# A change to the order of loads, small vector work and stream tiles in the up stage of one token block of an attention and SwiGLU kernel

## The chip, the cores and the metric

The kernel runs on one NeuronCore of a Trainium2 chip. The core has a matrix engine (TensorE, PE), a vector engine (VectorE, DVE), a scalar engine (ScalarE, ACT), GpSimd (POOL) and SyncE (SP). SP computes nothing here: it issues nearly all DMA transfers, one after another, and 16 DMA engines carry them. The metric is the device time of one execution in microseconds (us), the median of several runs. Lower is better.

## What is computed

An attention without softmax: for each batch and head k^T v is formed over the sequence, q is multiplied by it, and each row of 64 is normalised by its root mean square. Its output is regrouped to 4608 tokens of 512 and goes through a SwiGLU feed-forward block. All in float32.

```python
def _attn_ref(q, k, v, g_norm):            # 8 batches, 8 heads, 576 positions, 64 wide
    kv = np.einsum('bhsd,bhse->bhde', k, v)
    out = np.einsum('bhsd,bhde->bhse', q, kv)
    rms = np.sqrt(np.mean(out * out, axis=-1, keepdims=True) + 1e-06)
    return out / rms * g_norm

x = attn_out.transpose(0, 2, 1, 3).reshape(4608, 512)
g = x @ w_gate                             # 512 x 1536
silu = g * (1.0 / (1.0 + np.exp(-g)))
y = (silu * (x @ w_val)) @ w_out           # 1536 x 512
```

## The kernel before, in words

**Blocks.** The 4608 tokens are nine blocks of 512. An object `Att(n)` makes the input x of block n from q, k, v, and an object `Ffn(n)` carries it through an up stage (gate and value products), the SwiGLU product and a down stage. Nine blocks of 512 cover eight batches of 576, so block n needs the k^T v of batch n and of batch n - 1.

**Fast matrix products.** The large products use Strassen's scheme in Winograd's form: seven products of quarter blocks in place of eight, with sums of the operands before and of the products after. Block 0 multiplies plainly, while its weights arrive. Block 1 (`Up`) uses one level. Block 2 (`Inner`) and the pairs of blocks 3 and 4, 5 and 6, 7 and 8 (`Joint`) use two levels in the up stage, 49 leaf products, each named by an outer and an inner number such as (5, 1). The down stages (`Down`) use one level.

**Streamed weights.** Sums of weights (the leaves) are computed once in block 1 (`leaf_steps`, L922 and after) and written to a DRAM tile `w` by `send` (L932). Block 2 takes 16 of the 49 leaves straight from the gate and value weights that lie in SBUF (`RESIDENT`, `QUARTER`); the other 33 it streams from `w`. The pairs stream all 49. A stream tile is one buffer of `t_pool`, which has nine. `ALONE` (L841) lists in which tiles, and in which order, block 2 loads its leaves: 17 tiles for each of the three thirds d of the up stage. Where the leaves of a tile lie side by side in `w`, one transfer of 256 KB loads them (L894); otherwise two transfers of 128 KB do (L897). In the list before, 10 of the 17 tiles need two, which makes 27 transfers per third. `Stream.pump` (L878) adds a load whenever the ninth tile before it is free again.

**Queues.** The order of the instructions on each engine is settled when the kernel is built. The builder may move independent instructions past one another; `tc.issue_after` and `tc.keep_in_program_order` tie some of them. After that each engine works through its own list in order, and waits on semaphores where data or a buffer are not ready. For SP this means that a transfer that waits holds all transfers behind it.

**Units of the up stage of block 2.** Four units for each third (`Inner.GROUPS`: outers (1, 5), (6, 2), (7,), (4, 3)), twelve in all; units and tiles are counted from 0. In `Ffn.up` every unit runs its seven inner products; the last two of a unit (3 and 4) fall into the next one. After unit i the function `fill[i + 1]` is called: this is where attention work for later blocks is placed. `ahead` (L1230) makes this table for block 2. Products land in PSUM pools a, b, c (1, 3 and 2 buffers), and VectorE (L132) or ScalarE (L775) move them into ring tiles r.

**Attention work of block 3.** It consists of `load_kv(g)` (four transfers of 288 KB for half of the heads, L294), `kv(g)` (36 pairs of 64x64 matmuls, L344, then copies by ScalarE, L351), `load_quarters(i, pairs)` (q in pieces of 24 to 40 KB, L312; a block is 32 such pieces), `turn_q` (a transposition on VectorE, L359), `heads` (q times k^T v, L389), `squares` (squares on ScalarE, L402, and sums on VectorE, L403), `root` (the inverse root by an integer guess and three Newton steps on VectorE, L409 to L421), `scale` (L134), `turn_x` (transpositions on TensorE, L436, with copies on ScalarE, L437) and `sums` (four operand sums on VectorE). Loads of q, k and v share `ld_pool`, four buffers.

**Where it stands before.** k, v half 0 of block 3 is loaded at the end of block 1's up stage. All of q follows after block 1's down stage (`load_q`, L312). In `ahead`, unit 0 is followed by the first k, v product and the load of half 1; `turn` comes after unit 2, the second k, v product after unit 3, the halves of the attention product after units 4 and 7. k, v and q of block 4 are loaded in between. In the pairs, `fill` places the k, v products of the next two blocks after units 5 and 12, and the loads of their q after units 13 to 20.

Of the kernel before, what the change touches and what calls it, by code (L numbers as in the profile page):

```python
# [18 lines left out]
def kernel(  # L19
# [194 lines left out]
    class Att:  # L214
# [118 lines left out]
        def kv(self, g):  # L333
# [4 lines left out]
            if g == 0:  # L338
                self.kv_ps = [m_psum.tile([P, 2, D], F32, name="m") for _ in range(2)]
# [8 lines left out]
            if g == 1:  # L348
                dst = kvs[self.n % 3].rearrange("p (g r) d -> p r g d", r=2)
                for r in range(2):  # L350
                    nc.scalar.copy(out=dst[:, r], in_=self.kv_ps[r])  # L351
# [27 lines left out]

        def heads(self, i, pairs, pools=None):  # L380
# [14 lines left out]
        def squares(self, i):  # L395
            if self.z is None or 0 < self.n < TURNED:
                self.z = st_pool.tile([P, 2, 2, 2, NS], F32, name="z")
            if i == 0:
                self.sq = self.place("sq").rearrange("p f (t j d) -> p f t j d", t=2, j=NS)
            for u in range(2):  # L400
# [4 lines left out]
        def root(self, i, k=1):  # L405


# [9 lines left out]
            y, a, z = flat(y), flat(a), flat(z)  # L417
            for _ in range(3):
                nc.vector.scalar_tensor_tensor(out=a, in0=y, scalar=-0.5, in1=y, op0=OP.mult, op1=OP.mult)
                nc.vector.tensor_tensor(out=a, in0=a, in1=z, op=OP.mult)  # L420
                nc.vector.scalar_tensor_tensor(out=y, in0=a, scalar=1.5, in1=y, op0=OP.add, op1=OP.mult)  # L421

        def scale(self, i):
            if i == 0:
                self.xts = self.place("xts").rearrange("p (i t) (j u d) -> p i t j u d", i=2, j=NS, u=2)
            for u in range(2):
# [3 lines left out]
        def turn_x(self, i):  # L430
            xt = self.xts[:, i].rearrange("p t j u d -> p t j (u d)")
            for j in range(0, NS, 2):
                ps = m_psum.tile([P, 2, 2, P], F32, name="m")
                for e in range(2):
                    for t in range(2):
                        nc.tensor.transpose(ps[:, e, t], xt[:, t, j + e], ident)  # L436
# [31 lines left out]
        def sums(self):  # L468

            a11, a12, a21, _, s1, s3, s4 = (self.x[:, i] for i in range(7))  # L470
            add(nc.vector, s1, a21, self.x[:, 3])
            sub(nc.vector, s3, a21, a11)
            sub(nc.vector, a21, s1, a11)
            sub(nc.vector, s4, a12, a21)
# [332 lines left out]
    class Joint(Inner):  # L807
# [116 lines left out]

    def leaf_steps(j, sources, room):
# [8 lines left out]
        for t, os in sources:  # L934
# [9 lines left out]
            yield lambda t=t, os=os: send(os, (1, 6, 2, 3), t.rearrange("p o i e c -> p o (i e c)"))  # L944
# [93 lines left out]
    class Ffn:  # L1038
        def __init__(self, n, att):
# [4 lines left out]
            self.making, self.later, self.latest = [], [], []  # L1044
            self.visited = None
# [19 lines left out]
        def up(self, fill):  # L1065
# [11 lines left out]
            for i, this in enumerate(units):  # L1077
                if i + 1 < len(units):
                    units[i + 1].prepare()
                for unit, p in this.sequence(last):  # L1080
                    if unit:
# [3 lines left out]
                        self.make(4)  # L1085
                last = this
# [135 lines left out]
    def visit(ffn, att, gs):  # L1222

        with tc.issue_after(ffn.multiplied.ins):
            for g in gs:
                att.kv(g)
# [3 lines left out]
    def ahead(ffn, att):  # L1230

        def start():
            visit(ffn, att, (0,))
            att.load_kv(1)

        def turn():
            att.turn()
            blocks[PAIRED + 1].load_kv(0)

        def finish():  # L1240
            visit(ffn, att, (1,))
            blocks[PAIRED + 1].load_kv(1)

        def half(i):
            with tc.issue_after(ffn.multiplied.ins):
                att.half(i, (m_psum, m_psum))
            ffn.visited = att.multiplied

        def load(i):
            blocks[PAIRED + 1].load_quarters(i // 2, (i % 2,))  # L1250

        def second():
            visit(ffn, blocks[PAIRED + 1], (0, 1))
            load(0)

        def last():
            half(1)
            load(1)

        def turn_x(i):  # L1260
            with tc.issue_after(ffn.multiplied.ins):
                att.turn_x(i)
            load(2 + i)
            if i == 1:
                att.sums()
# [4 lines left out]
        }  # L1270
        return {
# [127 lines left out]
```

## Time and profile before

| | |
|---|---|
| three runs | 1039.46, 1039.88, 1041.76 us; median 1039.88 |
| profiled execution | 1040.75 us, of which 1039.0 from its first to its last instruction (the span) |
| mean granted TensorE clock | 0.989 of full speed |
| DMA | 155.2 MB in 261349 packets, 141968 of them under 512 bytes |
| SP's queue | 53.3% of the time of 16 DMA engines; ScalarE's queue 2.4% |
| stream loads | 198 of 256 KB, median 3.2 us from issue to landing; 117 of 128 KB, 3.5 us |
| k and v loads | 26 and 26 of 288 KB, median 5.5 and 6.5 us |
| chain that ended last | TensorE 70% of the span, DMA 3%, SP's queue 2%, VectorE 1% |

Block 1's down stage ends at about 270 us, block 2's up stage runs from there to 373 us and its down stage to 416 us; the three pairs take the rest. The chain that ended last goes back from the last instruction, at each step to what released it. Its shares are over the whole span, so a wait of some microseconds in one stage hardly shows in them; it shows in views cut to that stage. In those views a line names an engine, a source line, the operation, the tile written and the tiles read; in brackets is the idle time before it and what ended that.

### The profile page before, as it was taken

To read this page: it belongs to the slowest core of one execution; us is meant where nothing else is said; L and a number is where in the kernel's file an instruction comes from. 1 tells how busy PE (TensorE), PEld (TensorE's weight loads), DVE (VectorE), ACT (ScalarE), POOL (GpSimd) and SP (SyncE) were. 2 spreads that over 40 slices of the span, in tenths; PEclk is the share of its full clock that TensorE was granted. 3 is DMA by queue.
4 is the path that set the end of the run, shared out by engine and by line. 5 is a ranking of instruction groups with operands and counts; after the bars stand their busy time and mean duration, and the time that the engine had idled before them with its cause. 6 is when DMAs were issued, how large, how long until landed. Compare 5 with 4: busy or idle time off the path is not lost.

```text
span 1039.0 us, 17769 instructions
## 1 busy us (share of the span) xinstructions
PE 998.8 (96%) x6774; PEld 843.6 (81%) x6774; DVE 685.2 (66%) x1166; ACT 228.6 (22%) x355; POOL 359.6 (35%) x283
## 2 busy tenths in 40 slices
PE   6999999999948989999999999999999999999998
PEld 4544688888938978888878888888888888888887
DVE  3999688887726696656668557566685566676311
ACT  2765112221102211211121111221212112111100
POOL 0000263534004451255445301455552024656600
PEclk9999999999969999999999999999999999999999
DMA  8689633777889656584761555566603555543011
GB/s 233 207 257 256 127 67 138 246 229 175 255 187 224 155 140 142 159 218 133 187 162 47 127 103 159 144 180 177 146 11 73 112 155 161 147 144 108 1 41 41
DMA packets 261349, 155.20 MB, mean 149 GB/s; under 512 B 141968, under 2 KB 240528, under 8 KB 261264
## 3 DMA queue, kind: packets, MB, share of 16 engines
q1 hardware_dynamic: 230544, 150.13, 53.3%
q10 hardware_dynamic: 30656, 3.94, 2.4%
q8 instruction: 54, 0.88, 0.4%
q14 instruction: 31, 0.25, 0.1%
q0 software_dynamic: 64, 0.00, 0.0%
HBM read 117.97 MB, written 28.70 MB: 141 GB/s over the span
## 4 chain that ended last, share of the span: by engine, by line
PE 70%; DMA 3%; SPq 2%; DVE 1%; issue 0%; ACT 0%; DVEq 0%; ACTq 0%
PE b L761 23%; PE b L593 16%; PE c L761 11%; PE c L593 8%; PE a L761 6%; PE a L593 4%; DMA t<-w 2%; PE m L389 1%; PE m L344 1%; SPq L312 1%; DVE r L132 1%; DMA out_dram<-r 1%; SPq L897 0%; DVE arena L134 0%; SPq L294 0%
## 5 line engine op out<-in xcount | busy, mean ns | idle before, releaser
L761 PE MATMUL b<-arena,t 128*128 128x256 f32 (+1 forms) x1248 | 281.8, 365 | 21.9 <-DMA t<-w 15.3
L761 PEld LDWEIGHTS b<-arena,t 128*128 128x128 f32 x1248 | 223.1, 193 | 53.0 <-DMA t<-w 10.6
L132 POOL TENSOR_TENSOR r<-r 128x256 f32<-128x256 f32 (+1 forms) x105 | 110.5, 1054 | 333.2 <-DMA t<-w 148.7
L132 DVE TENSOR_TENSOR r<-b,r 128x512 f32<-128x512 f32 (+1 forms) x273 | 162.4, 606 | 77.1 <-PE b L761 72.1
L132 DVE TENSOR_TENSOR r<-c,r 128x512 f32<-128x512 f32 (+1 forms) x179 | 109.2, 618 | 98.0 <-PE c L761 48.7
L761 PE MATMUL c<-arena,t 128*128 128x256 f32 (+1 forms) x624 | 140.0, 362 | 0.7 <-ACT r L775 0.7
L133 POOL TENSOR_TENSOR t<-wo 128x512 f32<-128x512 f32 x54 | 77.4, 1458 | 167.5 <-DVE wo L132 104.4
L132 DVE TENSOR_TENSOR r<-a,r 128x512 f32<-128x512 f32 (+1 forms) x99 | 62.5, 631 | 107.9 <-PE a L593 66.6
L134 POOL TENSOR_TENSOR arena<-r 128x1024 f32<-128x1024 f32 (+1 forms) x46 | 96.1, 2103 | 87.7 <-DVE r L132 75.9
L761 PEld LDWEIGHTS c<-arena,t 128*128 128x128 f32 x624 | 111.9, 193 | 14.3 <-ACT r L775 1.2
L133 DVE TENSOR_TENSOR arena<-arena 128x512 f32<-128x512 f32 (+3 forms) x101 | 102.4, 1026 | 18.2 <-PE b L593 12.1
L593 PE MATMUL b<-wo,arena 128*128 128x256 f32 x432 | 98.8, 382 | 2.3 <-DVE arena L134 1.5
L593 PE MATMUL b<-t,arena 128*128 128x256 f32 x432 | 96.3, 380 | 0.0
L593 PEld LDWEIGHTS b<-wo,arena 128*128 128x128 f32 x432 | 81.1, 190 | 13.9 <-DVE arena L134 1.8
L593 PEld LDWEIGHTS b<-t,arena 128*128 128x128 f32 x432 | 82.0, 190 | 11.4 <-POOL s L132 0.2
L775 ACT COPY r<-b 128x512 f32<-128x512 f32 x63 | 36.9, 585 | 215.4 <-PE b L761 214.7
L761 PE MATMUL a<-arena,t 128*128 128x256 f32 (+1 forms) x288 | 72.6, 371 | 0.9 <-DMA t<-w 0.9
L761 PEld LDWEIGHTS a<-arena,t 128*128 128x128 f32 x288 | 53.5, 194 | 7.7 <-PE c L761 1.3
L788 ACT ACTIVATE r<-r 128x1024 f32<-128x1024 f32 x21 | 22.2, 1057 | 120.9 <-DVE r L132 120.9
L593 PE MATMUL a<-wo,arena 128*128 128x256 f32 x216 | 48.4, 379 | 0.0
L593 PE MATMUL c<-wo,arena 128*128 128x256 f32 x216 | 48.1, 379 | 0.0
L593 PE MATMUL c<-t,s 128*128 128x256 f32 x216 | 48.1, 379 | 0.0
(118 smaller groups left out, 1134.6 us busy)
## 6 DMA issues: line engine op xcount, KB each, us to landing
t<-w SPq DMA_DIRECT2D x198, 256.0 KB, 3.2
t<-w SPq DMA_DIRECT2D x117, 128.0 KB, 3.5
out_dram<-r SPq DMA_DIRECT2D x17, 512.0 KB, 2.9
ld<-in_k_dram SPq DMA_DIRECT2D x26, 288.0 KB, 5.5
ld<-in_v_dram SPq DMA_DIRECT2D x26, 288.0 KB, 6.5
ld<-in_moe_w_gate_dram SPq DMA_DIRECT2D x12, 512.0 KB, 4.9
ld<-in_moe_w_val_dram SPq DMA_DIRECT2D x12, 512.0 KB, 4.7
ld<-in_moe_w_out_dram SPq DMA_DIRECT2D x12, 512.0 KB, 4.7
```

The source lines that it names most:

```text
L132: add = lambda e, o, a, b: e.tensor_tensor(out=o, in0=a, in1=b, op=OP.add)
L133: sub = lambda e, o, a, b: e.tensor_tensor(out=o, in0=a, in1=b, op=OP.subtract)
L134: mul = lambda e, o, a, b: e.tensor_tensor(out=o, in0=a, in1=b, op=OP.mult)
L312: nc.sync.dma_start(out=to[32 * r : 32 * (r + 1), j, g0:g1], in_=q[b, 4 * i + 2 * j + h, s0 : s0 + 32 * (g1 - g0), 32 * d : 32 * (d + 1)]. ...
L344: self.positions = nc.tensor.matmul(self.kv_ps[r][u * D : (u + 1) * D, g, :], lhsT=k[:, u, c, :], rhs=v[:, u, c, :], start=(c == 0), stop= ...
L389: self.multiplied = nc.tensor.matmul(self.ps[i][u][p : p + D, t, j, :], lhsT=self.qt[rows, 2 * i + t, j, p : p + D], rhs=kvs[b % 3][rows, ...
L593: self.ffn.multiplied = nc.tensor.matmul(banks[e][:, e], lhsT=lhsT, rhs=rhs, start=first and i == 0 and (e == 0 or banks[0] is not banks[1 ...
L761: self.ffn.multiplied = nc.tensor.matmul(to, lhsT=weight, rhs=self.operand(o, p), start=begins, stop=True, skip_group_check=True,)
L775: nc.scalar.copy(out=dst, in_=ps)
L788: nc.scalar.activation(out=c11, in_=c11, func=ACT.Silu)
```

## The change

Block 3's k, v half 1 is loaded at the end of block 1 in place of q. In block 2's up stage the table of `ahead` is new: both k, v products of block 3 after unit 0 (`visits`), its q in four parts after units 0 to 3, the k, v halves of block 4 loaded after units 1 and 4 and multiplied separately after units 4 and 10 (`apart`), the attention product's halves after units 5 and 7, the q of block 4 in four parts after units 5 to 8. VectorE's small steps are put in a list, `chores`, of which one is taken after every inner product: the transpositions of q, squares, root and scale, and the sums of x. `ALONE` groups the leaves so that 14 of its 17 tiles load with one transfer: 20 transfers per third. Four of the leaf writes of 512 KB (base leaves of the last two of six weight groups) go to a list `owed_sends` and are issued after unit 10. In the pairs `fill` places the k, v products after units 4 and 10 and the q loads after units 11 to 18.

```diff
@@ -330,12 +330,12 @@
-        def kv(self, g):
+        def kv(self, g, apart=False):
-            if g == 0:
+            if g == 0 or apart:
                 self.kv_ps = [m_psum.tile([P, 2, D], F32, name="m") for _ in range(2)]
...
-            if g == 1:
+            if g == 1 or apart:
                 dst = kvs[self.n % 3].rearrange("p (g r) d -> p r g d", r=2)
+                of = slice(g, g + 1) if apart else slice(0, 2)
                 for r in range(2):
-                    nc.scalar.copy(out=dst[:, r], in_=self.kv_ps[r])
+                    nc.scalar.copy(out=dst[:, r, of], in_=self.kv_ps[r][:, of])
@@ -377,6 +378,15 @@
+        def chores(self, i):
+            yield lambda: self.squares(i, (0,))
+            yield lambda: self.squares(i, (1,))
+            yield from self.root_steps(i)
+            for u in range(2):
+                yield lambda u=u: self.scale(i, (u,))
@@ -392,18 +402,28 @@
-        def squares(self, i):
+        def squares(self, i, us=(0, 1)):
-            if i == 0:
+            if i == 0 and us[0] == 0:
                 self.sq = self.place("sq").rearrange("p f (t j d) -> p f t j d", t=2, j=NS)
-            for u in range(2):
+            for u in us:
                 sq = self.sq[:, 2 * i + u]
                 self.squared = nc.scalar.activation(out=sq, in_=self.ps[i][u], func=ACT.Square)
                 self.summed = nc.vector.tensor_reduce(out=self.z[:, i, u], in_=sq, axis=mybir.AxisListType.X, op=OP.add)
         def root(self, i, k=1):
+            for step in self.root_steps(i, k):
+                step()
+        def root_steps(self, i, k=1):
+            yield lambda: self.guess(i, k)
+        def guess(self, i, k):
...
+            self.near = flat(y), flat(a), flat(z)
+        def refine(self):
+            y, a, z = self.near
+            nc.vector.scalar_tensor_tensor(out=a, in0=y, scalar=-0.5, in1=y, op0=OP.mult, op1=OP.mult)
+            nc.vector.tensor_tensor(out=a, in0=a, in1=z, op=OP.mult)
+            nc.vector.scalar_tensor_tensor(out=y, in0=a, scalar=1.5, in1=y, op0=OP.add, op1=OP.mult)
+        def scale(self, i, us=(0, 1)):
...
-            for u in range(2):
+            for u in us:
                 y = self.y[:, i, u].unsqueeze(3).to_broadcast([P, 2, NS, D])
                 self.scaled = mul(nc.vector, self.xts[:, i, :, :, u], self.ps[i][u], y)
@@ -433,7 +456,7 @@
-                        nc.tensor.transpose(ps[:, e, t], xt[:, t, j + e], ident)
+                        self.turned_x = nc.tensor.transpose(ps[:, e, t], xt[:, t, j + e], ident)
@@ -467,11 +490,16 @@
         def sums(self):
+            for step in self.sum_steps():
+                step()
+        def sum_steps(self):
             a11, a12, a21, _, s1, s3, s4 = (self.x[:, i] for i in range(7))
-            add(nc.vector, s1, a21, self.x[:, 3])
-            sub(nc.vector, s3, a21, a11)
-            sub(nc.vector, a21, s1, a11)
-            sub(nc.vector, s4, a12, a21)
+            yield lambda: add(nc.vector, s1, a21, self.x[:, 3])
+            yield lambda: sub(nc.vector, s3, a21, a11)
+            yield lambda: sub(nc.vector, a21, s1, a11)
+            yield lambda: sub(nc.vector, s4, a12, a21)
@@ -839,9 +867,9 @@
     ALONE = (
-        ((5, 1), (5, 6)), ((1, 5), (5, 5)), ((5, 2), (5, 3)), ((1, 7), (5, 7)), ((2, 5), (6, 5)), ((1, 4), (5, 4)),
-        ((2, 7), (6, 7)), ((7, 1), (7, 6)), ((7, 7), (7, 5)), ((2, 4), (6, 4)), ((7, 2), (7, 3)), ((4, 1), (4, 6)),
-        ((4, 5), (3, 5)), ((7, 4),), ((4, 2), (4, 3)), ((4, 7), (3, 7)), ((4, 4), (3, 4)),
+        ((5, 1), (5, 6)), ((1, 5), (5, 5)), ((5, 2), (5, 3)), ((5, 7), (5, 4)), ((1, 7), (1, 4)), ((2, 5), (6, 5)),
+        ((6, 7), (6, 4)), ((2, 7), (2, 4)), ((7, 1), (7, 6)), ((7, 5),), ((7, 2), (7, 3)), ((7, 7), (7, 4)),
+        ((4, 1), (4, 6)), ((4, 5), (3, 5)), ((4, 2), (4, 3)), ((4, 7), (4, 4)), ((3, 7), (3, 4)),
     )
@@ -922,6 +950,8 @@
+    owed_sends = []
     def leaf_steps(j, sources, room):
...
-            yield lambda t=t, os=os: send(os, (1, 6, 2, 3), t.rearrange("p o i e c -> p o (i e c)"))
+            base = lambda t=t, os=os: send(os, (1, 6, 2, 3), t.rearrange("p o i e c -> p o (i e c)"))
+            if os[0] in RESIDENT and j >= NP - 2:
+                owed_sends.append(base)
+            else:
+                yield base
             yield lambda b11=b11, t2_=t2_, to=to: sub(nc.vector, to[:, :, 0], b11, t2_)
             yield lambda to=to, os=os: send(os, (7, 4, 5), to.rearrange("p o r c -> p o (r c)"))
@@ -1042,6 +1076,7 @@
+            self.chores = []
@@ -1083,6 +1118,8 @@
                         with tc.issue_after(visited.ins) if visited else ExitStack():
                             unit.multiply(p)
                         self.make(4)
+                        if self.chores:
+                            self.chores.pop(0)()
                 last = this
                 fill.get(12 * (i + 1) // len(units), lambda: None)()
@@ -1219,58 +1256,60 @@
-    def visit(ffn, att, gs):
+    def visit(ffn, att, gs, apart=False):
         with tc.issue_after(ffn.multiplied.ins):
             for g in gs:
-                att.kv(g)
+                att.kv(g, apart)
         if att.n < B:
             ffn.visited = att.positions
-    def ahead(ffn, att):
-        def start():
-            visit(ffn, att, (0,))
-            att.load_kv(1)
+    def ahead(ffn, att, then):
+        def visits():
+            visit(ffn, att, (0, 1))
+            att.load_quarters(0, (0,))
+        def second():
+            att.load_quarters(0, (1,))
+            then.load_kv(0)
         def turn():
-            att.turn()
-            blocks[PAIRED + 1].load_kv(0)
-        def finish():
-            visit(ffn, att, (1,))
-            blocks[PAIRED + 1].load_kv(1)
+            visit(ffn, then, (0,), True)
+            then.load_kv(1)
+            ffn.chores += [lambda i=i: att.turn_q(i) for i in range(2)]
         def half(i):
             with tc.issue_after(ffn.multiplied.ins):
-                att.half(i, (m_psum, m_psum))
+                att.heads(i, range(NS), (m_psum, m_psum))
             ffn.visited = att.multiplied
-        def load(i):
-            blocks[PAIRED + 1].load_quarters(i // 2, (i % 2,))
-        def second():
-            visit(ffn, blocks[PAIRED + 1], (0, 1))
-            load(0)
-        def last():
-            half(1)
-            load(1)
+            ffn.chores += att.chores(i)
+            then.load_quarters(i, (0,))
         def turn_x(i):
             with tc.issue_after(ffn.multiplied.ins):
                 att.turn_x(i)
-            load(2 + i)
+            ffn.visited = att.turned_x
             if i == 1:
-                att.sums()
+                ffn.chores += att.sum_steps()
+        def last():
+            visit(ffn, then, (1,), True)
+            while owed_sends:
+                owed_sends.pop(0)()
...
         }
+        def again(i):
+            then.load_quarters(i, (1,))
         return {
-            1: start, 3: turn, 4: finish, 5: lambda: half(0), 7: second, 8: last, 9: lambda: turn_x(0),
-            10: lambda: turn_x(1),
+            1: visits, 2: second, 3: lambda: att.load_quarters(1, (0,)), 4: lambda: att.load_quarters(1, (1,)),
+            5: turn, 6: lambda: half(0), 7: lambda: again(0), 8: lambda: half(1),
+            9: lambda: (turn_x(0), again(1)), 10: lambda: turn_x(1), 11: last,
         }
@@ -1316,7 +1355,7 @@
-            ffn.up(ahead(ffn, nxt))
+            ffn.up(ahead(ffn, nxt, blocks[PAIRED + 1]))
@@ -1325,8 +1364,7 @@
         if n == 1:
-            for i in range(2):
-                blocks[PAIRED].load_q(i)
+            blocks[PAIRED].load_kv(1)
@@ -1351,9 +1389,9 @@
-            fill = {6: first_kv, 13: second_kv}
+            fill = {5: first_kv, 11: second_kv}
             for i in range(8):
-                fill[14 + i] = lambda i=i, after=after: after[i // 4].load_quarters(i % 4 // 2, (i % 2,))
+                fill[12 + i] = lambda i=i, after=after: after[i // 4].load_quarters(i % 4 // 2, (i % 2,))
```

More of the change, by code (lines that the diff above doesn't have):

```diff
@@ L405, in root @@
         def root(self, i, k=1):
+            for step in self.root_steps(i, k):
+                step()
+        def root_steps(self, i, k=1):
+            yield lambda: self.guess(i, k)
+            for _ in range(3):
+                yield self.refine
+        def guess(self, i, k):
             z = self.z[:, i : i + k]
@@ L416, in root @@
             flat = lambda t: t.rearrange("p i u t j -> p (i u t j)")
[L417 to L424, printed above, removed]
+            self.near = flat(y), flat(a), flat(z)
[5 more added lines that the diff above has]
+        def scale(self, i, us=(0, 1)):
+            if i == 0 and us[0] == 0:
                 self.xts = self.place("xts").rearrange("p (i t) (j u d) -> p i t j u d", i=2, j=NS, u=2)
-            for u in range(2):
+            for u in us:
                 y = self.y[:, i, u].unsqueeze(3).to_broadcast([P, 2, NS, D])
```

## The prediction

> **What bounds the kernel now.** I read the page's first two parts, then one call of busy time by stretches, the waits of TensorE, the timelines of SP and TensorE, and the rows of the stream loads. The page:
>
> ```profile
> PE 998.8 (96%) x6774; PEld 843.6 (81%) x6774; DVE 685.2 (66%) x1166; ACT 228.6 (22%) x355; POOL 359.6 (35%) x283
> ...
> PE   6999999999948989999999999999999999999998
> PEclk9999999999969999999999999999999999999999
> ```
>
> TensorE is busy 96% of 1039.0 us, and the two slices in which it is not lie at 285 to 310 us, where the clock falls too. That is the up stage of block 2, from 270 to 373 us, the stage that the diff rewrites. Busy time by stretches there (PE, weight loads, DVE, ACT, POOL, then clock, DMA share, GB/s):
>
> ```profile
> 270.00:285.00 15.00, 14.51 (x189) 14.13 (x187) 9.15 (x15) 2.34 (x4) 1.59 (x3) 1.00 0.78 235
> 285.00:310.00 25.00, 9.29 (x45) 8.78 (x46) 6.16 (x9) 1.06 (x1) 1.32 (x2) 0.59 0.79 182
> 310.00:329.00 19.00, 19.00 (x284) 18.62 (x283) 12.07 (x24) 4.92 (x9) 10.07 (x6) 1.00 1.10 250
> 329.00:340.00 11.00, 7.61 (x175) 7.20 (x174) 6.19 (x13) 1.49 (x3) 2.43 (x4) 0.84 0.60 168
> 340.00:361.00 21.00, 21.00 (x243) 20.81 (x242) 15.40 (x33) 6.71 (x11) 10.58 (x7) 1.00 0.63 148
> 361.00:373.00 12.00, 9.69 (x80) 9.09 (x79) 11.86 (x21) 1.26 (x2) 3.98 (x4) 1.00 0.77 188
> ```
>
> Idle is 103 minus 81.1 busy, or 21.9 us. What ended it, by TensorE's waits from 270 to 373 us:
>
> ```profile
> PE b L761 <- DMA t<-w: 15.3, 2, 10.4
> PE b L761 <- DVE r L132: 6.6, 5, 3.4
> ```
>
> Two waits for streamed weights, five for VectorE's evacuations. SP's queue says why the weights were late:
>
> ```profile
> 275.98 0.43 SPq L1049 DMA_DIRECT2D out_dram<-r  x1
> 276.47 17.26 SPq L312 DMA_DIRECT2D ld<-in_q_dram  x30
> 293.82 0.92 SPq L897 DMA_DIRECT2D t<-w  x2
> ```
>
> Thirty q loads of block 3 stand in one row, and the tenth weight tile of the stage is issued only behind them. TensorE meanwhile:
>
> ```profile
> 296.52 2.20 PE L761 MATMUL b<-arena,t 128*128 128x128 f32 x8 [10.44 <-DMA t<-w]
> ...
> 305.33 1.19 PE L761 MATMUL b<-arena,t 128*128 128x128 f32 x4 [4.89 <-DMA t<-w]
> ...
> 332.69 2.81 PE L761 MATMUL b<-arena,t 128*128 128x128 f32 x12 [3.39 <-DVE r L132]
> ```
>
> Eight matmuls took 2.20 us after the first wait, where the full clock makes 8 x 0.1115 = 0.9.
>
> **The floor of the stage.** 588 matmul instructions of 128x128 at 0.1115 us (1.79 us for 16 in the chain of waits) are 65.6 us; four k,v products of 72 at 1.28 or half of 2.26 make 4.8; two attention products of 1.16, 2.3; two transpositions of x at 0.9, 1.8. Sum 74.5 us against 103: **28.5 us are excess**, of which 21.9 is idle and about 6.5 the halved clock. After 416 us TensorE waits 2.0 us in all, and block 2's down stage loses about 1.5; neither is what the diff is about.
>
> **What the Trainium skill says.** "TensorE: Matmul & The Clock Gate", Part 1 (the HAM clock gate): after an idle window of about 3.4 us the array drops to half clock and needs about as long a busy stretch to return. The trace agrees: 0.59 mean clock after the 10.44 us wait, 0.84 after the 3.39 us one. So a wait near 3.4 us costs some 2 us more than itself. "DMA: Bandwidth & Descriptors", Anatomy of one DMA: a semaphore wait happens on the issuing sequencer before dispatch. So one load whose buffer isn't free holds all SP loads behind it; the row above shows such a queue. Same page, Rules for kernel authors: under 64 KB a transfer is mostly overhead. The q loads are 24 to 40 KB, and in their row the DMA moved 67 GB/s (busy time by stretches, 285 to 295 us).
>
> **The change part by part.**
>
> *q of block 3 out of the row (gain).* In the built order SP has, behind the nine tiles issued in block 1's down stage, three k,v loads, two tiles, eight q loads, four tiles (five transfers), eight q, four k,v, four tiles (five transfers), eight q, four tiles, eight q, and so on. The wall is gone, so the 10.44 and 4.89 us waits and their clock (2.0 + 1.8 us by the two stretched groups) have no cause left in this form. Removed: 15.3 + 0.9 + about 4 = **20 us**.
>
> *Fewer stream transfers (gain on SP).* 27 transfers a third become 20, 21 fewer in all at 0.42 us plus a gap of 0.05, **10 us of SP time**, and the halves of 512 B runs become 1 KB runs.
>
> *What SP must still do.* 64 q loads at 0.50 (the undisturbed part of the row: 0.49 from start to start) = 32; 11 k,v loads at 0.63 = 7; the 49 stream transfers behind the first nine tiles at 0.47 = 23; four 512 KB leaf writes at 0.5 = 2. Sum **64 us beside 74.5 of TensorE**. It fits on the whole, but not early: q of block 3 and k,v of block 4 stand in the first third.
>
> *The early shortage (cost).* The second output store can't leave before VectorE's last addition of block 1, which ended at 272.2 us. Then k,v to 274.1, two tiles to 275.1. The first q needs the ld buffer that k,v product 0 frees at 275.8. Eight q to 279.8, five transfers to 282.2, eight q to 286.2, four k,v to 288.7: tile 15, leaves (4,7) and (4,4), is issued there and lands 4.5 us later by the median of the rows of such loads (2.2 to 7.3), at 293.2. TensorE wants it at 269.9 + 4.5 (unit 0) + 1.3 + 6.2 (unit 1) + 1.3 + 4.0 + 4.5 = 291.7. Late by 1.5 at the median, 4.3 at the slowest. The next third's (5,2), behind eight more q, is issued at 295.1 and wanted at 297.2 but there at about 300: 2.8 late in all, some 6 when loaded, and four 288 KB loads just ahead do load the DMA. By the end of unit 5 SP has caught up. I take **4 us** (bounds 1.5 to 9).
>
> *k,v half 1 of block 3 (cost).* Half of the loads stand behind the same store, issued 272.2 to 274.1, landing by the 5 to 6 us of such loads at 278 to 280; the product is now right behind unit 0 and unit 1's first steps, about 278.5. **1 us** (0 to 2).
>
> *The norm in steps (gain and cost).* The same operations are issued: per half two reductions of 0.6, eleven small ones of about 0.2, two products of 0.65, but one piece behind each product instead of a run. The run at 322 to 332 us made the 3.39 us wait and 2 us of lost clock; the sums (0.6 and 1.0 us each) and block 4's transposition made 2.3 more. VectorE is 63% busy in the stage, so spread pieces can hide; but in the built order the root's last steps and scale still stand in one run ahead of evacuations, because reductions wait for ScalarE's squares, which wait for the product. Of 7.7 us I leave **3** (bounds 0 to 7).
>
> *Second and last third (cost).* SP brings 8 q, 5 transfers per unit of 6.2 us: 6.4 us. It has no reserve; k,v half 1 of block 4 waits for VectorE to turn q. **2 us** (0 to 6). Clock after such waits: **2** (0 to 4).
>
> *Leaf writes moved to unit 11, fills at 5 and 11 in the pairs, x sums spread, the T tiles on POOL earlier.* The four 512 KB writes leave a stretch with DMA share 0.9 to 1.0 for the end, where the share is 0.77; their readers are 20 us away. In the pairs SP and TensorE have slack (2.0 us of waits in 620 us). 0 (-1 to +2).
>
> Kept excess: 4 + 1 + 3 + 2 + 2 = 12 of 28.5. Gain **16.5 us**. The profiled execution took 1040.75 for a span of 1039.0, so 1024.25 there; it lies 0.9 above the median 1039.88, so about 1023.5, and I say **1024**. With all lower bounds 1.5 us stay: 1013; with all upper ones 28 + 2 stay, just over before. The upper ends can't all come at once easily, as a wait for one covers the other.
>
> **Rivals.**
> *Everything hides*: excess 1 to 5 us, 1013 to 1018. For it: 9 tiles of reserve, and the stretch from 310 to 329 us ran with DMA at 1.10 and TensorE full. Against: SP's early sum above. 0.2.
> *SP takes TensorE's place as the bound*: while eight transfers with a slow store among them were in flight, the first seven q took 6.1 us, 0.87 each. At 0.87 for all 64, SP needs 64 + 24 = 88 us, and with 5 us before and behind the stage lasts 93: gain 4 to 10, 1030 to 1036. 0.18.
> *Slower*: the loop of buffers. A load on SP waits for VectorE to turn q, VectorE waits for q behind SP, TensorE for both, and each turn of it costs a landing of 4.5 us plus cold clock. It decides from an SP need of 98 us (103 less those 5), which is 1.03 for each q load; at 1.1 the stage lasts 70 + 32 + 5 = 107 us, and the kernel 1044. Against: two groups of loads wait for VectorE in this way, and q of block 3 is wholly issued before the first of them. 0.08.
> *Nothing gained*: the shortage only moves to other tiles, 1038 to 1042: 0.05.
>
> **How the numbers follow.** Main case (1018 to 1030) 0.49, hides 0.2, SP-bound 0.18, nothing 0.05, slower 0.08. Faster by over 0.2% (2 us, what a measurement here can tell): 0.49 + 0.2 + 0.18 = 0.87, less a little for the edge, 0.86; within 0.05; slower 0.09. The range 1013.5 to 1037 leaves out slower, nothing and the best edge.
>
> **What would show it.** Right: no idle over 5 us in the stage, SP's timeline with q in eights, stream waits of 3 to 6 us near 290 to 300 us, clock near 1.00. Wrong: a new wait for k,v or t<-w over 10 us, waits of VectorE for q that pass to TensorE, or the stage over 95 us long.

## The result, and the profile after

The changed kernel takes 1033.56 us at the median of 8 runs (1031.11 to 1040.35), before 1040.1 on the same chip. The ratio is 0.9947 (95% interval 0.9923 to 0.9971), or 5.5 us of 1040 (the medians lie 6.5 us apart), where 16.5 were forecast. The profiled execution took 1036.02 us for a span of 1034.2.

The page of the changed kernel, TensorE's busy time, its slices and its clock:

```profile
PE 1002.4 (97%) x6774; PEld 847.2 (82%) x6774; DVE 684.0 (66%) x1166; ACT 228.9 (22%) x357; POOL 360.4 (35%) x283
...
PE   5999999999978889999999999999999999999998
...
PEclk9999999999998989999999999999999999999999
```

The deepest slice of before (4 in TensorE's row) is gone, but four slices of 7 or 8 stand in the same stage in its place. Busy time by stretches, in the columns and at the borders shown of before:

```profile
270.00:285.00 15.00, 15.00 (x240) 14.33 (x239) 6.88 (x10) 2.87 (x6) 0.24 (x1) 1.00 0.74 181
285.00:310.00 25.00, 19.59 (x157) 18.88 (x159) 12.12 (x21) 3.87 (x5) 8.73 (x7) 0.93 0.82 200
310.00:329.00 19.00, 16.36 (x241) 15.54 (x241) 13.72 (x32) 3.05 (x6) 6.39 (x7) 0.91 0.85 203
329.00:340.00 11.00, 11.00 (x136) 10.78 (x137) 6.21 (x16) 2.84 (x5) 2.37 (x1) 0.84 0.84 218
340.00:361.00 21.00, 18.22 (x214) 17.14 (x213) 16.52 (x28) 5.44 (x9) 13.20 (x10) 1.00 0.81 241
361.00:373.00 12.00, 6.92 (x38) 6.90 (x39) 10.09 (x11) 0.00 (x0) 5.50 (x3) 0.72 0.66 170
```

From 285 to 310 us TensorE is busy 19.6 us, before 9.3: the two walls of waits are gone. But from 361 to 373 us it is busy 6.9 us at 0.72 of the clock, before 9.7 at 1.00. The up stage of block 2 ends at 372.67 us, before at 372.60: most of what was won in its first third was given back at its end. TensorE's waits in the stage, from its timeline:

```profile
299.36 2.83 PE L789 MATMUL b<-arena,t 128*128 128x128 f32 x12 [3.23 <-DMA t<-w]
308.85 1.13 PE L789 MATMUL b<-arena,t 128*128 128x128 f32 x8 [2.18 <-DMA t<-w]
324.06 1.16 PE L789 MATMUL b<-arena,t 128*128 128x128 f32 x8 [0.30 <-DVE r L132]
328.89 0.71 PE L789 MATMUL b<-arena,t 128*128 128x128 f32 x4 [2.34 <-DVE r L132]
343.07 0.71 PE L789 MATMUL a<-arena 128*128 128x128 f32 x4 [1.52 <-DVE r L132]
366.07 1.22 PE L789 MATMUL b<-arena,t 128*128 128x128 f32 x4 [6.27 <-DVE r L132]
```

The first two are the early shortage, the next three stand behind the norm's work on VectorE, and the last, 6.27 us, the largest of the stage, was in no term of the forecast. VectorE's timeline shows what it was doing ahead of the evacuation (the move of a product from PSUM into a ring tile) at 365.01 us, for which TensorE waited:

```profile
357.63 1.24 DVE L132 TENSOR_TENSOR arena<-arena 128x896 f32<-128x896 f32 x1
358.80 6.29 DVE L133 TENSOR_TENSOR arena<-arena 128x896 f32<-128x896 f32 x3
365.01 1.01 DVE L132 TENSOR_TENSOR r<-b,r 128x256 f32<-128x256 f32 x2
```

These four sums of 896 columns are block 3's `inner_sums`, which nothing reads before block 3's own products at 412 us. In before the builder set them between evacuations from 367 to 377 us, as VectorE's timeline there shows:

```profile
367.07 1.08 DVE L132 TENSOR_TENSOR arena<-arena 128x896 f32<-128x896 f32 x1
368.07 1.09 DVE L133 TENSOR_TENSOR arena<-arena 128x896 f32<-128x896 f32 x1
...
373.54 1.83 DVE L133 TENSOR_TENSOR arena<-arena 128x896 f32<-128x896 f32 x1
...
375.89 1.56 DVE L133 TENSOR_TENSOR arena<-arena 128x896 f32<-128x896 f32 x1
```

In the changed order they stand in one run, and each of the last three took 2.03 to 2.15 us. Beside them GpSimd made its T tiles (differences of blocks of w_out for the down stage), which in before it began only at 373.15 us:

```profile
357.89 6.25 POOL L133 TENSOR_TENSOR t<-wo 128x512 f32<-128x512 f32 x3
```

Outside of the stage, the profiled execution won 3.0 us in block 2's down stage (42.7 to 39.7 us) and 1.85 from block 3's first product to the end (623.7 to 621.9). Of the 3.0, 1.1 was a wait for VectorE; 0.9 are eight matmuls of the up stage (before had 16 left over when its down stage began, the changed kernel 8); 1.0 I can't place.

### The profile page after: what moved, and what is told of

It reads as the page before. It is cut to its first block, busy times and chain, and to the rows that moved or that the text cites. A ratio compares the mean times of both kernels' runs of the same rounds, so it can differ in the third digit from the quotient of the medians.

```text
span 1034.2 us, 17746 instructions
## 1 busy us (share of the span) xinstructions
PE 1002.4 (97%) x6774; PEld 847.2 (82%) x6774; DVE 684.0 (66%) x1166; ACT 228.9 (22%) x357; POOL 360.4 (35%) x283
## 4 chain that ended last, share of the span: by engine, by line
PE 74%; DMA 2%; DVE 1%; issue 0%; ACT 0%; SPq 0%; DVEq 0%; ACTq 0%
PE b L789 25%; PE b L621 16%; PE c L789 12%; PE c L621 8%; PE a L789 6%; PE a L621 4%; PE m L344 1%; PE m L399 1%; DMA t<-w 1%; DVE r L132 1%; DMA ld<-in_k_dram 1%; PE m L459 0%; DVE arena L134 0%; PE b L399 0%; PE a L399 0%
## 5 line engine op out<-in xcount | busy, mean ns | idle before, releaser
L621 PEld LDWEIGHTS a<-wo,arena 128*128 128x128 f32 x216 | 41.1, 190 | 5.5
```

The source lines that it names most:

```text
L621: self.ffn.multiplied = nc.tensor.matmul(banks[e][:, e], lhsT=lhsT, rhs=rhs, start=first and i == 0 and (e == 0 or banks[0] is not banks[1 ...
```

## The experiments

All times below are medians; the ratio to before is the fair comparison, as before took 1039.4 to 1041.1 us beside them. "Up and down" is block 2's up and down stage together in the profiled execution, from the first product of the one to the first product of block 3; that execution can lie some us off the median (1036.0 for the changed kernel).

| kernel | us | ratio to before, 95% | up and down, us |
|---|---|---|---|
| before | 1039.9 | 1 | 145.4 |
| changed | 1033.6 | 0.9947 (0.9923 to 0.9971) | 142.2 |
| sums behind the up stage | 1030.0 | 0.9906 (0.9893 to 0.9919) | 135.8 |
| T tiles later | 1028.8 | 0.9894 (0.9881 to 0.9906) | 134.1 |
| sums where VectorE is idle | 1024.1 | 0.9852 (0.9837 to 0.9867) | 131.7 |
| norm whole | 1034.7 | 0.9952 (0.9936 to 0.9967) | 139.7 |
| old transfers | 1036.9 | 0.9971 (0.9961 to 0.9981) | 141.8 |
| old leaf writes | 1036.3 | 0.9966 (0.9953 to 0.9979) | 141.2 |
| old fills in the pairs | 1035.7 | 0.9952 (0.9936 to 0.9968) | 139.2 |
| new places alone | 1044.2 | 1.0046 (1.0030 to 1.0062) | 148.4 |
| new places alone, sums moved | 1035.6 | 0.9948 (0.9937 to 0.9960) | 140.2 |
| sums moved, q on two queues | 1023.4 | 0.9844 (0.9829 to 0.9859) | 127.7 |
| sums moved, k, v one unit later | 1027.3 | 0.9862 (0.9847 to 0.9877) | 133.2 |
| sums moved, k, v two units later | 1023.9 | 0.9836 (0.9824 to 0.9849) | 128.8 |

The theory, T1: the missing gain is lost in the tail, where the hoisted sums stand ahead of an evacuation. Rivals: SP's queue is the bound (T2), or the norm's steps delay the evacuations (T3).

**Sums behind the up stage.**

```diff
-        ffn.down(nxt, {1: blocks[PAIRED].inner_sums} if n == 2 else {})
+        def late_sums(ffn=ffn):
+            with tc.issue_after(ffn.ended.ins):
+                blocks[PAIRED].inner_sums()
+        ffn.down(nxt, {1: late_sums} if n == 2 else {})
```

> The changed kernel (1033.6 us at the median) with one thing altered: block 3's four inner sums (128x896, VectorE) are queued behind VectorE's last sum of block 2's up stage instead of in one run ahead of the last evacuations. The same operations are done. Theory T1 (most of the missing gain is lost in the last 13 us of the stage, where these sums, slowed to twice their time by the T tiles on GpSimd, hold an evacuation for which TensorE waits 6.27 us and then runs 5 to 6 us at about half clock): that wait falls below 2 us, the stage is 7 to 11 us shorter, 1023 to 1027 us. Rival T2 (SP's queue is the bound: q loads at 0.62 to 0.88 us each): what is won at the end is small, since the last weights are late anyway, 1031 to 1034. Rival T3 (the norm's steps ahead of evacuations): as T2, 1031 to 1034.

The 6.27 us wait is gone and the up stage takes 91.6 us in place of 102.5, all that T1 asked of it. But the time fell by 4.3 us only (0.0041 of 1040). The down stage took 44.2 us instead of 39.7. VectorE, ScalarE and TensorE of this kernel, from their timelines:

```profile
368.98 1.08 DVE L132 TENSOR_TENSOR arena<-arena 128x896 f32<-128x896 f32 x1
369.99 4.91 DVE L133 TENSOR_TENSOR arena<-arena 128x896 f32<-128x896 f32 x2
...
386.46 6.81 ACTq L482 DMA_DIRECT2D arena<-r  x8
393.31 0.59 ACT L1049 COPY r<-b 128x512 f32<-128x512 f32 x1 [16.76 <-DMA arena<-r]
...
394.04 7.11 PE L621 MATMUL b<-t,arena 128*128 128x256 f32 x24 [2.57 <-ACT r L1049]
```

Two sums took 4.91 us, again with T tiles beside them, just ahead of block 4's norm. So block 4's x was ready later, ScalarE stood at the eight transfers that place it, and TensorE waited 2.57 us for the copy behind them and then took 7.11 us for what takes 5.34. A stall moved out of one chain was put into another.

**T tiles later.** GpSimd's three tiles of `turn_t(5)` queued behind its own last addition; the sums stay in their run.

```diff
-                add(nc.gpsimd, self.whole(1, 0), self.whole(2, 0), self.whole(0, 1))
+                self.ffn.pooled = add(nc.gpsimd, self.whole(1, 0), self.whole(2, 0), self.whole(0, 1))
...
-            self.down_.turn_t(5)
+            with tc.issue_after(self.pooled.ins) if self.n == DEEP else ExitStack():
+                self.down_.turn_t(5)
```

> The changed kernel with the three T tiles that GpSimd makes at the end of block 2's up stage queued behind GpSimd's own addition of the last unit; the four inner sums stay in one run ahead of the evacuation. It parts the two halves of T1, the order from the shared slowing. If VectorE and GpSimd slow each other there, the sums take about 1.05 us each again in place of 2.0 to 2.15, TensorE's wait of 6.27 us falls to about 3, and the time is 1028 to 1031 us; if the order alone did it, the sums stay at 2 us and the time at 1032 to 1035. T2 and T3: 1032 to 1035. It could lose 1 to 3 us in the down stage, whose first products use these tiles.

VectorE's sums and TensorE's wait in this kernel:

```profile
353.83 3.33 DVE L133 TENSOR_TENSOR arena<-arena 128x896 f32<-128x896 f32 x3
...
358.15 0.71 PE L789 MATMUL b<-arena,t 128*128 128x128 f32 x4 [3.32 <-DVE r L132]
```

The same three sums take 1.11 us each instead of 2.1, and the wait is 3.32 us instead of 6.27, as expected. About half of the wait was the order, half the neighbour; the time fell by 5.5 us (0.0053). The Trainium skill states this, "SBUF — State Buffer", section "Who interferes with whom": a VectorE instruction with two SBUF inputs contends with a GpSimd instruction that reads SBUF, and the port pair that they share is an exclusive lock. Both engines agree with it here: GpSimd's tiles too took 2.11 us each beside the sums and 1.26 where nothing stood beside them.

**Sums where VectorE is idle.** Queued behind the transposition of block 4's x, after which VectorE waited 9.84 us for TensorE.

```diff
-                nc.vector.transpose(
+                self.blocked = nc.vector.transpose(
...
+        def late_sums(att=nxt):
+            with tc.issue_after(att.blocked.ins):
+                blocks[PAIRED].inner_sums()
```

> The changed kernel with block 3's four inner sums queued on VectorE behind the transposition of block 4's x in block 2's down stage, where VectorE stood idle for 9.8 us; GpSimd's T tiles stay where they are. T1, as it stands after the sums queued behind the last sum of the up stage (the tail's wait fell from 6.27 us to nothing and the up stage from 102.5 to 91.6 us, but the down stage grew from 39.7 to 44.2, since the same sums then held block 4's norm): no 6 us wait at the end of the up stage, and no 2.6 us wait for ScalarE in the down stage; up 91 to 93 us, down 39.5 to 40.5, 1023 to 1027 us. Rival T4 (the tail's time is owed in any place, because something else, such as the k,v loads of block 5 or the last weights, is late there next): the up stage is again near 96 to 100 us and the time 1029 to 1033.

1024.1 us, 0.0095 below the changed kernel in the ratio, or 9.9 us, with the intervals far apart. Up took 92.0 us and down 39.7, both as T1 had them; the rival that the time is owed in any place falls. TensorE's waits in it:

```profile
299.27 2.84 PE L789 MATMUL b<-arena,t 128*128 128x128 f32 x12 [3.28 <-DMA t<-w]
308.49 1.13 PE L789 MATMUL b<-arena,t 128*128 128x128 f32 x8 [1.82 <-DMA t<-w]
323.74 1.16 PE L789 MATMUL b<-arena,t 128*128 128x128 f32 x8 [0.30 <-DVE r L132]
328.58 0.71 PE L789 MATMUL b<-arena,t 128*128 128x128 f32 x4 [2.33 <-DVE r L132]
341.28 0.71 PE L789 MATMUL a<-arena 128*128 128x128 f32 x4 [1.51 <-DVE r L132]
```

It is the changed kernel's list without its last line.

**Parts undone one at a time**: the norm issued whole, the old list `ALONE` (the minus lines of the change), the leaf writes, the fills.

```diff
-            ffn.chores += att.chores(i)
+            for step in att.chores(i):
+                step()
...
-            if os[0] in RESIDENT and j >= NP - 2:
+            if False:
...
-            fill = {5: first_kv, 11: second_kv}
+            fill = {6: first_kv, 13: second_kv}
...
-                fill[12 + i] = lambda i=i, after=after: after[i // 4].load_quarters(i % 4 // 2, (i % 2,))
+                fill[14 + i] = lambda i=i, after=after: after[i // 4].load_quarters(i % 4 // 2, (i % 2,))
```

In the first, `turn_q` and `sums` are issued whole in the same way.

> The changed kernel without the norm in steps: q's transposition, squares, root, scale and the x sums of block 3 are issued whole behind their product, as before the change; everything else of the change stays. T1: the steps were worth little or something, 1033 to 1038 us, with one or two waits of TensorE for VectorE of 2 to 4 us in the middle of the stage in place of the three of 0.3 to 2.3. T3 (the steps themselves put work ahead of the evacuations): faster, 1028 to 1032. T2: as now, 1032 to 1035.

> The changed kernel with the old list of weight transfers, 27 a third in place of 20. T2 (SP's queue is the bound): 21 transfers more at 0.47 to 0.7 us are 10 to 15 us on SP, most of it seen, 1042 to 1050 us. T1: SP has some slack outside of the first third; there 7 transfers more make the two stream waits of 3.23 and 2.18 us some 3 to 5 us longer in all, with 1 to 2 us of clock, 1037 to 1041. If the grouping is worth nothing: 1032 to 1035.

> The changed kernel with the base leaves of the last pair sent where they were before the change, not after the last k,v product. All theories: DMA was at 1.05 of its share in the tail with the late writes and k,v of block 5 together, so the writes back in their place can make the loads at 340 to 360 us later or the tail lighter: 1032 to 1036 us, within 2 us of the changed kernel. T2 (SP and DMA as the bound): slower, 1035 to 1038. Were the late writes part of the loss in the tail, 1029 to 1032 with the 6.27 us wait for VectorE shorter.

> The changed kernel with the pairs' loads of k, v and q at the joint units where they stood before the change (6, 13, 14 on). From the two traces: from block 3's first product to the end, before took 623.7 us and the changed kernel 621.9. If the fills made this, 1035 to 1036.5 us and two waits of 0.7 to 0.9 us return; if they made nothing, 1033 to 1034.5.

Against the changed kernel's 0.9947 the norm in steps and the fills in the pairs make no difference that these runs can tell (0.9952 both); the fills show only in the traces, where the stretch from block 3's first product to the end is 623.4 to 623.7 us in the four kernels with the old ones and 621.8 to 622.6 in the ten with the new. VectorE's timelines show why the steps make no difference: with the norm issued whole the builder sets its small operations between the evacuations in nearly the same order, and the run of the root's last steps and scale stays. The transfers are worth about 2.5 us (0.9971) and the late writes 2 (0.9966), yet the changed kernel's own interval, 2.5 us to each side, touches theirs. With the old writes a wait of 3.27 us for v stands at 284.57 us, which the changed kernel doesn't have. T3 is not borne out: TensorE then waits for VectorE 2.12 and 1.45 us at the same places, and 5.67 us in the tail.

**All four undone, and then with the sums moved.**

> The changed kernel with only the new places of the loads and products of blocks 3 and 4 kept: the old 27 transfers a third, the norm whole, the leaf writes and the pairs' fills as before the change. If the parts add (whole norm +1.1 us, old transfers +3.4 us over the changed kernel's 1033.6): 1037 to 1040 us, so that the new place of q alone is worth 0 to 2 us, not the 20 that the removed waits made it. If the new place is worth what the removed waits were and is only lost in the tail: 1031 to 1036. If the old transfers and the whole norm stand in each other's cover: 1040 to 1044.

> The new places of the loads and products alone (old transfers, whole norm, old leaf writes and fills: 1044.2 us), with block 3's inner sums behind the transposition of x. T1: the 5.62 us wait and its halved clock at the end of the up stage go here too, 8 to 10 us less, 1034 to 1036 us: the new places alone then gain 4 to 6 us over before, and their order at the end hid it. If the tail is owed for another reason (late transfers), 1040 to 1044.

The new places of loads and products alone are slower than before by 4.8 us. Two of TensorE's waits in that kernel:

```profile
283.17 1.02 PE L344 MATMUL m<-ld 64*64 64x64 f32 x26 [2.62 <-DMA ld<-in_v_dram]
...
371.19 1.22 PE L789 MATMUL b<-arena,t 128*128 128x128 f32 x4 [5.62 <-DVE r L132]
```

So the tail's run of sums comes with the new places, not with the norm's steps or the fills. What in the new places makes the builder set the sums there was not looked into. Moving the sums there wins 10.2 us too (1.0046 to 0.9948), and the places alone then gain 5.4 us over before. The four parts, each worth at most 2.5 us when undone alone, are worth 10.3 together (1.0046 less 0.9947), and 10.0 with the sums moved (0.9948 less 0.9852). That each covers some of what the others leave late would explain it; it was not shown.

**What is left of the early shortage (T2).** Half of block 3's q loads on ScalarE's queue; or block 4's first k, v loads one or two units later.

```diff
-                            nc.sync.dma_start(
+                            queue = nc.scalar if self.n == PAIRED and r % 2 else nc.sync
+                            queue.dma_start(
```

The other two take `then.load_kv(0)` out of `second`:

```diff
+        def third():
+            att.load_quarters(1, (0,))
+            then.load_kv(0)
...
+        def fourth():
+            att.load_quarters(1, (1,))
+            then.load_kv(0)
...
+        def sixth():
+            visit(ffn, then, (0,), True)
+            then.load_kv(1)
+            half(0)
```

the one by `third` after unit 2, the other by `fourth` after unit 3, and there the visit and `then.load_kv(1)` move from `turn` to `sixth`, after unit 5.

> As the kernel with the inner sums behind the transposition of x, and with half of block 3's q loads (16 of 32) issued on ScalarE's queue in place of SP's. T2 in its remaining form (SP's queue makes the weights of the first third late, 3.23 and 2.18 us of waits and some 3 us of halved clock): SP gains 10 us there, these waits go, and the kernel is 4 to 8 us faster than its partner. If the landing of the loads themselves (transfers shared by all queues) makes the weights late, or ScalarE's copies now stand behind its q loads: from 1 us faster to 4 us slower than its partner.

> The kernel with the inner sums behind the transposition of x (1024.1 us), and with the four k,v loads of block 4's first half one unit later on SP, behind eight more q loads and the next tiles. T2 in its remaining form (the weights of the first third are issued too late): tile 15 is issued 2.6 us earlier, the wait of 3.28 us falls below 1 us and its halved clock goes, the next one of 1.82 stays: 1020 to 1023. If the landing is what is late, the wait stays at 2.5 to 3.5 us: 1023 to 1025. If k and v then come late for their product behind unit 5: 1025 to 1028.

> As the one before, with these four loads two units later, and the product of block 4's first k,v half and the loads of its second half behind unit 6 in place of 5. T2: both stream waits (3.28 and 1.82 us) fall below 1 us, 1018 to 1021. If the landing is what is late: 1022 to 1025. If the loads of the second half, now 6 us later, come late for their product in the last third: 1024 to 1029.

None of the three is told apart from its partner at 0.9852. With q on two queues SP and TensorE show:

```profile
295.20 3.45 SPq L923 DMA_DIRECT2D t<-w  x3
...
299.24 0.71 PE L790 MATMUL b<-arena,t 128*128 128x128 f32 x4 [3.06 <-DMA t<-w]
```

SP issued tile 15 at 295.20 us, later than the changed kernel's 293.62, though eight loads fewer stood ahead of it: the first wait stays. The second, 1.82 us in the partner, isn't in this trace. (The table's 127.7 us against 131.7 for the partner comes from the fastest execution of the one and the slowest of the other.) "DMA: Bandwidth & Descriptors", section "Issuing engines are not separate DMA queues", says that a second queue saves only the sequencer's time, and the times agree (0.9844 against 0.9852). With k, v later the wait moved rather than shrank:

```profile
308.71 1.22 PE L789 MATMUL a<-arena,t 128*128 128x128 f32 x4 [5.82 <-DMA t<-w]
```

in the one by one unit, and in the one by two:

```profile
312.03 1.81 PE L789 MATMUL b<-arena,t 128*128 128x128 f32 x8 [4.21 <-DMA t<-w]
```

The changed kernel's SP timeline shows the rate:

```profile
276.20 7.07 SPq L312 DMA_DIRECT2D ld<-in_q_dram  x8
...
285.88 5.00 SPq L312 DMA_DIRECT2D ld<-in_q_dram  x8
290.92 1.26 SPq L294 DMA_DIRECT2D ld<-in_k_dram  x2
292.28 1.25 SPq L294 DMA_DIRECT2D ld<-in_v_dram  x2
293.62 1.57 SPq L922 DMA_DIRECT2D t<-w  x3
```

Eight q loads take 5.0 to 7.1 us, 0.62 to 0.88 each. In the traces each transfer waits, besides its own buffer, on one of eight completion semaphores taken in turn, and so for the landing of the transfer eight before it; with q on two queues both take from the same eight. SP's waits by releaser bear this out, with q held by landings of weights that it doesn't read:

```profile
SPq L312 <- DMA t<-w: 6.9, 15, 2.0
```

A landing of 5.3 us, the median of q, k and v from 270 to 284 us, by eight in flight is 0.66 us a load. In the two rows above 16 loads at 0.49 us, the step from start to start where none waits, would be 7.8 us; the other 4 are such waits. So what came on top of the forecast is the landing, not SP's own work, which speaks against T2 as it was put. What a larger number in flight would bring was not tried.

## Why the prediction was wrong

The direction was right, and so was the main source of the gain, the row of q loads. By its own steps, in the profiled execution:

- *q of block 3 out of the row*: the waits of 10.44 and 4.89 us are gone. But the new places alone gain 5.4 us, not 20, even with the tail mended: without the new transfers and writes other waits come for k, v and for weights.
- *The early shortage*, 4 us: 5.41 us (3.23 and 2.18), and two stretches at half clock behind them, 3.4 us. Tile 15 was issued at 293.62 where 288.7 was worked out, because q took 0.62 to 0.88 us and not 0.50 each; the row that gave 0.50 was one in which DMA had little else to do. The tile landed at 299.3, 6 us after the 293.2 worked out, but TensorE came for it only at 296.1, 4.4 us after the 291.7: that the first wait lies near the forecast is in part luck.
- *k,v half 1 of block 3*, 1 us: 1.25, but not from a late load (see the last section).
- *The norm in steps*, 3 us: 4.2 us in three waits, with the root's last steps and scale in one run ahead of evacuations, as foreseen, and 1.7 us of clock. The steps themselves had no part in it: two of these waits are 2.12 and 1.45 us with the norm whole. (VectorE's 63% is 59% by the prediction's own table.) *Second and last third*, 2 us: no wait for weights after 310 us.
- *Clock after such waits*, 2 us: 7.7 us over the stage, summed from 1 us slices as busy time by 1 less the clock; 2.6 of it belongs to the tail. This term is too small without the tail too: it counts on waits near 3.4 us, and waits of 2.18 and 2.34 us halved the clock as well (last section).
- *Leaf writes moved to unit 11, fills at 5 and 11 in the pairs, x sums spread, the T tiles on POOL earlier*, 0 (-1 to +2): **this is the step that failed.** It priced earlier T tiles at nothing without a reason and didn't ask what VectorE does beside them; and the inner sums of block 3, whose place moved without a line of the diff naming them, were in no term at all. Together they are 6.27 us of wait and 2.6 of halved clock. Moving the sums alone gave 9.9 us, and the kernel with them moved takes 1024.1 us.

The prediction kept 12 us above its floor of 74.5 us for the stage; the stage of 102.5 us kept 28.0. The terms above make 24.8 of them, the rest I can't place. Of the 12.8 us by which these terms passed the forecast, 8.9 are the tail and 3.1 the clock elsewhere.

That the kernel with the sums moved lands on the forecast 1024 is in part chance: its up stage is 10.7 us shorter than before's, not 16.5, and 4.5 more come from the down stage and the pairs, which were held to give nothing. Of the signs named for wrong one came, a stage of over 95 us. VectorE never waited for q in it; it made TensorE wait for another reason. The likeness in time with the rival *SP takes TensorE's place as the bound* (1030 to 1036) is chance too: that rival's cause, tried three ways, moved the time by at most 1.7 us either way.

The scatter of the changed kernel, 1031 to 1040 us, is larger than of any kernel with the tail mended (at most 3.7 us). The granted clock goes with it: 0.990 to 0.992 in the three executions above 1036 us, 0.993 to 0.995 in the five at 1034 or below. That the same short waits halve the clock in some executions and not in others would do this; it was seen across kernels (last section), not between executions of one. Two kernels with the tail as it was scatter by only 1.7 and 2.3 us.

## What to carry to other kernels

When a change moves work through a scheduler, compare the built order of every engine from the first moved instruction to the next stage, and look for unnamed work that has become a run ahead of an evacuation. A sum that nothing reads for 40 us belongs where its engine idles: queue it behind the last step of the chain that it could delay, not merely behind the stage that it has left. Additions on VectorE and GpSimd that both read SBUF at the same time are to be priced at about twice their time (here 2.1 us in place of 1.11 and 1.26).

## What the hardware showed unexpectedly

**A wait of about 2 us can halve the clock, and need not: it depends on where it falls.** The traces hold every change of the granted clock. In each of the fourteen all changes lie on one grid of 3.41 us, and every stretch at half clock between is one or more whole steps of it. The grid lies differently against each execution's start. Two waits of the same place and length, 2.34 us in the changed kernel and 2.33 in the one with the sums moved, ended at 328.9 and 328.6 us. The step that holds most of the wait, and the one behind it (clock third from the end), in the first:

```profile
326.93:330.34 3.41, 1.45 (x13) 1.45 (x14) 2.69 (x6) 0.00 (x0) 0.00 (x0) 1.00 0.59 167
330.34:333.76 3.42, 3.42 (x19) 3.42 (x18) 1.54 (x3) 0.00 (x0) 2.37 (x1) 0.50 0.90 204
```

and in the second:

```profile
327.01:330.42 3.41, 1.84 (x16) 1.84 (x17) 2.69 (x5) 0.00 (x0) 0.00 (x0) 1.00 0.75 220
330.42:333.84 3.42, 3.42 (x54) 3.22 (x57) 2.17 (x5) 0.00 (x0) 2.35 (x1) 1.00 0.78 164
```

TensorE was busy 1.45 us of the step (42%) in the first and 1.84 (54%) in the second, where the step's border had left more of the wait outside. I counted 3792 steps at full clock, from 60 to 1000 us of the fourteen traces. All 31 in which TensorE was busy 45% or less were followed by half clock, none of those with 53% or more; between these, five of seven were. The waits of 2.18 and 1.82 us left 36% and 47% and halved it, those of 1.5 us left 56% or more and did not. "TensorE: Matmul & The Clock Gate", section "What's actually happening", calls its window of about 3.4 us free-running, and the grid agrees. Its table has the clock drop after an idle window; here a window that was busy for 42% sufficed.

**The same 72 small products take twice as long when not interleaved.** Block 3's two k, v halves in the changed kernel:

```profile
274.83 1.28 PE L344 MATMUL m<-ld 64*64 64x64 f32 x72
...
278.91 1.27 PE L344 MATMUL m<-ld 64*64 64x64 f32 x36
280.75 1.26 PE L344 MATMUL m<-ld 64*64 64x64 f32 x36
```

Half 0 alternates between the two halves of the partitions (r of 0 and 1 in `kv`). For half 1 the builder set all of one and then all of the other, with an inner product between: 36 alone take as long as 72 in turn, which costs 1.25 us. The starts in the trace show it: in half 0 four products start together every 58 ns, in half 1 two.
